# Retention, Mish layer and GELU layer in one kernel: from unit 7 on, the scores of two units stand in a row

## The chip, the cores and the metric

The kernel runs on one core of a Trainium2 chip. The metric is device time in microseconds (us) of one launch, the median of several runs. The engines are named as in the profile: PE (TensorE's matmuls) and PEld (its weight loads), DVE (VectorE), ACT (ScalarE), POOL (GpSimd) and SP (SyncE, which issues the DMAs).

## The reference, cut to what matters

```python
scores = scale * np.matmul(q, k.transpose(0, 1, 3, 2))      # B, H, S, D = 4, 8, 576, 64
...
Dmat = np.where(rel >= 0, gamma[:, None, None] ** rel[None, :, :], 0.0)
ret = scores * Dmat[None, :, :, :]
return np.matmul(ret, v).astype(np.float32)
...
h = x @ w_in                                                # 2304 x 512 by 512 x 2048
g = h * np.tanh(sp)                                         # Mish
return (g @ w_out).astype(np.float32)
...
g = h * (1.0 / (1.0 + np.exp(-1.702 * h)))                  # the second layer, same sizes
return (g @ w_out).astype(np.float32)
```

A retention (attention with a decay in place of a softmax), and behind it two feed-forward layers. The change is in the retention alone.

## The kernel before, in words

**Units.** Retention is worked off in 20 units, numbered u = 0 to 19: four batches of five stretches of the sequence, four of 128 positions and a last one of 64 (the rests: units 4, 9, 14 and 19). A unit's q, k and v lie in one of six buffers (`unit` in the profile: three of the kernel's own with numbers 76 to 78, three lent by the layers that come later) or, for a rest, in `rest`. Within a batch a unit takes over a state from the unit before it.

**What PE does for a unit.** Four groups of eight float32 matmuls each, one per head. The profile counts 16 records for a group of eight.

- `sc` (L875, in `scores`): the products of q and k. They go to two PSUM banks, one for the even heads and one for the odd ones. A weight tile has 64 rows and 128 columns (64 and 64 for a rest).
- `ds` (L898, in `update`): the unit's addition to the state, summed in a bank that the units of a batch share. A rest has none. ACT copies the sum to `state` (in `take`) before the next unit may add to it.
- `o` from `state` (L926, in `outputs`): what the state of before gives. The first unit of a batch has none.
- `o` from `pm` (L938, in `outputs`): masked scores times v. The `ds` and `o` groups have weight tiles of 128 rows and 64 columns, but for the last group of a rest, which has 64 and 64.

**What the other engines do for a unit.** DVE multiplies the two banks of scores with a causal mask into two tiles `pm` (L879, the masks: two instructions); a unit's banks are free for other scores when its masks have read them. When `o` is complete DVE multiplies it with a table into `X` (L956, in `finish`). Between these DVE stands in the service of the coming layers: it splits `X` into two parts (L403), and converts weights (L202, L142, L214, L250), with ACT and POOL. All engines work off their instructions in the order of the program.

**Banks.** Scores take turns in four banks, two per unit (`bank("sc", (0, 1, 2, 3))`). So the scores of unit u+2 use the banks of unit u.

**The order.** It is written out by hand in the loop over u in `attention`: from unit 4 on a step of the loop issues the scores and masks of u+1, then `ds` of u, `o` of u, `finish` of u, and then what is planned of conversions. At the end of steps 17 and 18 the first products of the next layer (`h`, L416) are issued.

Of the kernel before, what the change touches and what calls it, by code (L numbers as in the profile page):

```python
# [25 lines left out]
CH = [(c, min(P, S - c)) for c in range(0, S, P)]  # L26
NCH = len(CH)
UNITS = [(b, c) for b in range(B) for c in range(NCH)]
# [19 lines left out]
LAG = 3  # L48

KEPT = (0, 1, 2, 3, 4, 8, 9, 10, 11, 12)  # L50
X_UNITS = (4, 5, 6, 7, 10, 11, 12, 13)
EARLY_AT = ((2, 8), (7, 13))
EARLY = len(EARLY_AT)
# [47 lines left out]
def retention_mish_gelu_kernel(ctx: ExitStack, tc: tile.TileContext, qkv, w1, w2, first_unit, rests, out):  # L101
# [23 lines left out]
    def bank(kind, of):  # L125
        taken[kind] = taken.get(kind, -1) + 1
        return ps.tile([P, NB], F32, tag=f"b{of[taken[kind] % len(of)]}", name=kind)

    def quarters(t):
        return t.rearrange("p (c n) -> p c n", c=NPAIR)  # L130

    def act(o, i, f=AF.Copy, scale=1.0, bias=0.0):
        nc.scalar.activation(out=o, in_=i, func=f, scale=scale, bias=bias)  # L133
# [18 lines left out]
    def plan(name, step, job):  # L152
        plans.setdefault(name, []).append((step, job))
        plans[name].sort(key=lambda p: p[0])

    def position(name, step):
        for j in [j for j in under_way if j[1] == name]:
            j[1] = next(j[0], None)
            if j[1] is None:
                under_way.remove(j)  # L160
        while plans.get(name) and plans[name][0][0] <= step:
            job = plans[name].pop(0)[1]
            then = next(job, None)
            if then:
                under_way.append([job, then])
# [8 lines left out]
    def place(m):  # L174
        return keep if m in KEPT else late[0]

    def fetch(m):

        r, h = divmod(m, 2)
        for i in range(2):  # L180
            if h == 0:
                at = RAW[i, r]
                held[i, r] = place(at).tile([P, 4, DM // 2], I64, tag=f"w{at}", name="raw")
            nc.sync.dma_start(
                out=held[i, r][:, 2 * h : 2 * h + 2],
                in_=w1[m][:, i * DM : (i + 1) * DM].rearrange("p (q n) -> p q n", q=2),
            )
        return
        yield
# [173 lines left out]
    n_u = len(UNITS)  # L363
# [12 lines left out]
    for m, s in zip(range(EARLY, NM), LATE):  # L376
        here = m < NM - 2 and all(RAW[i, m // 2] in KEPT and RAW[i, m // 2] not in LENT for i in range(2))
        plan("fetch", s - 2.5 if here else max(s - 2.5, 0), fetch(m))
# [417 lines left out]
    def attention():  # L796
        with tc.tile_pool(name="att", bufs=1) as ap:
# [11 lines left out]
            def load(u):  # L809

                b, c = UNITS[u]
                if c == NCH - 1:
                    t = ap.tile([P, LAST], F32, tag="rest", name="rest", bufs=2)
                    nc.sync.dma_start(out=t, in_=rests[b])
                    loaded[u] = views(t, REST)
                    return
                t = buffers[(u - b) % len(buffers)]
                if u == 0:
                    for e0, e in ((0, 2 * DM), (2 * DM, FIRST)):
                        nc.sync.dma_start(out=t[:, e0:e], in_=first_unit[:, e0:e])  # L820
                else:
                    for e in (0, 2 * DM) if u == 1 else (0,):
                        e1 = e + 2 * DM if u == 1 else 4 * DM
                        nc.sync.dma_start(out=t[:, e:e1], in_=qkv[b, c, :, e:e1])
                loaded[u] = views(t, P)
# [34 lines left out]
            def decay_v(u):  # L860
                b, c = UNITS[u]
                n = CH[c][1]
                vv = loaded[u][2][:n].rearrange("p (h d) -> p h d", d=D)
                for eng, h, e in ((nc.vector, 0, SPLIT), (nc.gpsimd, SPLIT, H)) if u == 0 else ((nc.gpsimd, 0, H),):
                    by = vt[:n, c, h:e].unsqueeze(2).to_broadcast([n, e - h, D])
                    eng.tensor_tensor(out=vv[:, h:e], in0=vv[:, h:e], in1=by, op=ALU.mult)

            def scores(u):
                n = CH[UNITS[u][1]][1]
                qt, kt = loaded[u][:2]  # L870
                sc = [quarters(bank("sc", (0, 1, 2, 3))) for _ in range(2)]
                for p in range(NPAIR):
                    for j in range(2):
                        sl = slice(64 * j, 64 * j + 64)
                        nc.tensor.matmul(sc[j][:n, p, :n], lhsT=kt[sl, p, :], rhs=qt[sl, p, :], start=True, stop=True)  # L875
                pm[u] = []
                for j in range(2):
                    t = ap.tile([P, NPAIR, P], F32, tag="pm", name="pm", bufs=4)
                    nc.vector.tensor_tensor(  # L879
                        out=t[:n, :, :n],  # L880
                        in0=sc[j][:n, :, :n],
                        in1=cm[:n, :n].unsqueeze(1).to_broadcast([n, NPAIR, n]),
                        op=ALU.mult,
                    )
                    pm[u].append(t)

            def update(u):

                c = UNITS[u][1]
                if c == NCH - 1:  # L890
                    return
                v, kk = loaded[u][2:]
                if c == 0:
                    sums[0] = quarters(bank("ds", (4, 5)))
                for p in range(NPAIR):
                    for j in range(2):
                        sl = slice(p * P + 64 * j, p * P + 64 * j + 64)
                        nc.tensor.matmul(  # L898
                            sums[0][64 * j : 64 * j + 64, p, :D],
                            lhsT=kk[:, sl],  # L900
                            rhs=v[:, sl],
                            start=(c == 0 and p == 0),
                            stop=True,
                            skip_group_check=True,
                        )

            def take(u):

                if UNITS[u][1] == NCH - 1:
                    return None  # L910
                for j in range(2):
                    sl = slice(64 * j, 64 * j + 64)
                    act(state[u % 2][sl, :, sl], sums[0][sl, :, :D])
                return state[u % 2]
# [55 lines left out]
            for u in range(n_u):  # L970
                step = u - n_u
                if u - 1 in wide and wide.index(u - 1) + len(buffers) < len(wide):
                    n = wide[wide.index(u - 1) + len(buffers)]
                    load(n)
                    if n + 1 not in wide:
                        load(n + 1)
                if u + 1 < n_u:
                    decay_v(u + 1)
                position("pool", step)
                position("fetch", step)  # L980
                if u == 0:
                    for n in wide[NCH : len(buffers)]:
                        load(n)
                if NCH - 1 <= u < n_u - 1:
                    scores(u + 1)
                before = now[0]

                def step_state():
                    update(u)
                    now[0] = take(u)  # L990

                if u != 1:
                    step_state()
                o = outputs(u, before, *((step_state,) if u == 1 else ()))
                if 0 < u < NCH - 1:
                    scores(u + 1)
                if u < NCH - 1:
                    n = CH[u + 1][1]
                    for p in range(NPAIR):
                        act(gt[:, u + 1, p, :n], gt[:, 0, p, :n], scale=steps[:, p, u + 1 : u + 2])  # L1000
                position("act early", step)

                if u == n_u - 2:
                    elementwise(0, jobs=False)
                finish(u, o)
                if u == n_u - 1:
                    elementwise(1, jobs=False)
                if u == 0:
                    scores(1)
                position("vector", step)  # L1010
                position("act late", step)
                if u in X_UNITS:
                    k = X_UNITS.index(u)
                    split_x((0, SIDE)[k // NK], k % NK)()
                if u == n_u - 3:
                    up(0)
                if u == n_u - 2:
                    up(1)
# [266 lines left out]
```

## Time and profile before

| what | value |
|---|---|
| median of 3 runs | 807.77 us (807.33 to 807.77) |
| the profiled execution | 807.27 us, of which 805.6 us are its span |
| PE busy | 800.3 us, 99% of the span |
| DVE busy | 585.9 us, 73% |
| ACT, POOL busy | 446.3 us, 55%; 190.3 us, 24% |
| retention on PE | from 4.8 us to 70 us of the span |
| PE's idle time that another engine ended | 0.5 us at the first `ds`, 0.4 us at 480 us |

The share of busy time is a mean over stages. For the retention alone the stretch from 13 to 70 us has to be looked at; in the 25 us from 35 to 60 DVE is as busy as PE. A PE that is busy all the time has not the same speed all the time: how long a group of matmuls takes from its first start to the first start of the next group is read from the order of time.

### The profile page before, as it was taken

The page shows a single profiled execution, that of the slowest core. Times are in us where ns is not written, and L with a number is a line of the kernel's source. Part 1 is how long each engine was busy: PE and PEld are TensorE (multiplying, and loading weights), DVE is VectorE, ACT ScalarE, POOL GpSimd, SP SyncE. Part 2 cuts the span into 40 slices and gives each one's busy share as a digit, 9 for nine tenths or more (in the row PEclk, how much of TensorE's full clock was granted, in tenths as well). Part 3 has the DMA queues.
Part 4 walks back from the last instruction along what each step waited for, and adds up shares of the span by engine and source line. Part 5 has one row for each costly group of instructions (what it writes and reads, how often), then busy time and mean ns, then how long its engine had stood idle before and what let it go on. Part 6 is the DMA issues. An engine that isn't in the chain of part 4 may idle for free.

```text
span 805.6 us, 14286 instructions
## 1 busy us (share of the span) xinstructions
PE 800.3 (99%) x5394; PEld 760.9 (94%) x5394; DVE 585.9 (73%) x992; ACT 446.3 (55%) x861; POOL 190.3 (24%) x251
## 2 busy tenths in 40 slices
PE   9999999999999999999999999999999999999998
PEld 8998888889999999999999999999999999999998
DVE  4896999998687666577677376798555897656775
ACT  5455877766766665666566454664233663234542
POOL 3362322220376450366570051000000000000000
PEclk9999999999999999999999999999999999999999
DMA  9994578837789995698986699888888788888784
GB/s 367 416 376 132 192 266 277 279 127 245 276 298 332 311 318 177 210 325 309 346 284 217 206 347 382 272 273 266 298 252 256 249 273 287 280 251 257 254 267 161
DMA packets 92326, 219.68 MB, mean 273 GB/s; under 512 B 6497, under 2 KB 52577, under 8 KB 90465
## 3 DMA queue, kind: packets, MB, share of 16 engines
q1 hardware_dynamic: 92112, 218.56, 80.4%
q8 instruction: 43, 0.70, 0.3%
q14 instruction: 27, 0.21, 0.1%
q10 hardware_dynamic: 144, 0.20, 0.1%
HBM read 169.98 MB, written 48.76 MB: 272 GB/s over the span
## 4 chain that ended last, share of the span: by engine, by line
PE 98%; DVE 1%; DMA 1%; ACT 0%; issue 0%; SPq 0%
PE p L731 22%; PE p L682 21%; PE acc L1093 17%; PE p L1156 15%; PE h L416 8%; PE acc L437 8%; PE sc L875 2%; PE o L938 2%; PE o L926 2%; PE ds L898 1%; DMA unit<-first_unit_dram 1%; DVE cs L475 0%; DVE u L475 0%; DVE X L142 0%; ACT cs L133 0%; DVE cy L352 0%
## 5 line engine op out<-in xcount | busy, mean ns | idle before, releaser
L682 PE MATMUL p<-xop,ring 128*128 128x384 f32 x1008 | 175.6, 334 | 0.4 <-DVE cs L475 0.4
L682 PEld LDWEIGHTS p<-xop,ring 128*128 128x128 f32 x1008 | 174.6, 188 | 0.8 <-DVE cs L475 0.7
L731 PE MATMUL p<-g,ring 128*128 128x384 f32 x1008 | 175.2, 334 | 0.0
L731 PEld LDWEIGHTS p<-g,ring 128*128 128x128 f32 x1008 | 174.8, 188 | 0.0
L1093 PE MATMUL acc<-g,w 128*128 128x512 f32 (+1 forms) x768 | 143.8, 337 | 0.0
L1093 PEld LDWEIGHTS acc<-g,w 128*128 128x128 f32 x768 | 124.3, 188 | 17.1 <-DVE g L475 0.3
L1156 PE MATMUL p<-xop,ring 128*128 128x384 f32 x672 | 128.4, 337 | 0.0
L1156 PEld LDWEIGHTS p<-xop,ring 128*128 128x128 f32 x672 | 115.7, 188 | 0.3
L133 ACT ACTIVATE g<-cs 128x384 fp32r<-128x384 f32 x168 | 79.0, 517 | 60.3 <-PE p L731 60.0
L475 DVE TENSOR_TENSOR g<-cs,g 128x384 fp32r<-128x384 f32 x168 | 90.0, 553 | 26.7 <-ACT g L133 25.1
L133 ACT ACTIVATE cs<-cs 128x384 f32<-128x384 f32 x72 | 37.8, 526 | 104.6 <-DVE cs L475 104.6
L475 DVE TENSOR_TENSOR g<-c,g 128x384 fp32r<-128x384 f32 x64 | 44.0, 688 | 39.0 <-ACT g L133 38.2
L437 PE MATMUL acc<-g,w 128*128 128x512 f32 (+1 forms) x384 | 72.3, 337 | 0.0
L437 PEld LDWEIGHTS acc<-g,w 128*128 128x128 f32 x384 | 60.2, 190 | 7.6
L133 ACT ACTIVATE c<-p 128x384 f32<-128x384 f32 x64 | 31.3, 489 | 54.4 <-PE p L1156 54.0
L218 POOL TENSOR_TENSOR raw<-raw 128x512 int32<-128x512 int32 x32 | 37.2, 1161 | 97.1 <-DVE raw L214 85.6
L133 ACT ACTIVATE g<-c 128x384 fp32r<-128x384 f32 (+1 forms) x96 | 50.5, 526 | 12.4 <-PE acc L437 9.9
L342 POOL TENSOR_TENSOR cy<-cy 128x128 f32<-128x128 f32 x88 | 54.9, 634 | 5.2
L475 DVE TENSOR_TENSOR cs<-cs 128x384 f32<-128x384 f32 x96 | 53.4, 556 | 0.8
L133 ACT ACTIVATE raw<-raw 128x512 int32<-128x512 uint32 x64 | 42.1, 680 | 16.7 <-DVE raw L202 16.7
L416 PE MATMUL h<-x,w 128*128 128x512 f32 x192 | 46.4, 391 | 0.0
L218 POOL TENSOR_TENSOR cy<-cr 128x256 int32<-128x256 int32 x38 | 31.2, 842 | 62.0 <-DVE cr L214 57.4
(93 smaller groups left out, 963.4 us busy)
## 6 DMA issues: line engine op xcount, KB each, us to landing
ring<-stream SPq DMA_DIRECT2D x168, 512.0 KB, 4.6
ring<-first_stream SPq DMA_DIRECT2D x56, 512.0 KB, 5.3
stream<-cy SPq DMA_DIRECT2D x22, 896.0 KB, 5.2
raw<-w_dram SPq DMA_DIRECT2D x32, 512.0 KB, 8.3
unit<-qkv_dram SPq DMA_DIRECT2D x14, 1024.0 KB, 13.7
cr<-w_dram SPq DMA_DIRECT2D x19, 512.0 KB, 5.7
stream<-X SPq DMA_DIRECT2D x10, 896.0 KB, 5.3
first_stream<-cy SPq DMA_DIRECT2D x16, 512.0 KB, 3.3
```

Of the source, the lines that this page charges most:

```text
L133: nc.scalar.activation(out=o, in_=i, func=f, scale=scale, bias=bias)
L218: nc.gpsimd.tensor_tensor(out=o, in0=upper, in1=bits, op=ALU.add)
L342: nc.gpsimd.tensor_tensor(out=v[:, o], in0=v[:, a], in1=v[:, b], op=op)
L416: nc.tensor.matmul(h[:, :n], lhsT=W[0, m // 2][:, m % 2, a, k * P : (k + 1) * P], rhs=xs[t, k][:, b, :n], start=((k, a, b) == order[0]), s ...
L437: nc.tensor.matmul(acc[t, e][:, :n], lhsT=W[1, m // 2][:, m % 2, a, e * P : (e + 1) * P], rhs=g[:, b, :n],  start=(begins(i) and a == 0 an ...
L475: eng.tensor_tensor(out=o, in0=a, in1=b, op=op)
L682: nc.tensor.matmul(banks[p], lhsT=w[:, k, a * P : (a + 1) * P], rhs=x[:, b, k], start=(p not in SAME and k == 0 and a == 0 and b == 0), st ...
L731: nc.tensor.matmul(banks[e, p], lhsT=w[:, e, a * P : (a + 1) * P], rhs=g[:, b], start=(p != 2 and r == 0 and a == 0 and b == 0), stop=(r = ...
L875: nc.tensor.matmul(sc[j][:n, p, :n], lhsT=kt[sl, p, :], rhs=qt[sl, p, :], start=True, stop=True)
L926: nc.tensor.matmul(o[sl, p, :n], lhsT=before[:, p, sl], rhs=qt[:, p, :], start=(p == 0), stop=True, skip_group_check=True,)
L1093: nc.tensor.matmul(acc[t, e][:, :w], lhsT=W[1, m // 2][:, m % 2, a, e * P : (e + 1) * P], rhs=g[:, b, o : o + w], start=(m == 0 and a == 0 ...
L1156: nc.tensor.matmul(bank, lhsT=w[:, a, k * P : (k + 1) * P], rhs=x[:, b, k], start=(p in (1, 2, 7) and k == 0 and a == 0 and b == 0), stop= ...
```

## The change

`scores` is split into products and masks. From step 7 on every second step issues the products and masks of unit u+1 and at once the products of unit u+2; the step behind it issues only the masks of its u+1 (whose products are there already). So the products of units 8 and 9 stand in a row, then those of 10 and 11, and so on to 18 and 19: six pairs. Behind each pair the `ds` and `o` groups of two units follow one another.

```diff
+PAIRS_FROM = 7
...
-            def scores(u):
+            products = {}
+
+            def scores(u, mask=True):
                 n = CH[UNITS[u][1]][1]
                 qt, kt = loaded[u][:2]
-                sc = [quarters(bank("sc", (0, 1, 2, 3))) for _ in range(2)]
+                sc = products[u] = [quarters(bank("sc", (0, 1, 2, 3))) for _ in range(2)]
                 for p in range(NPAIR):
                     for j in range(2):
                         sl = slice(64 * j, 64 * j + 64)
                         nc.tensor.matmul(sc[j][:n, p, :n], lhsT=kt[sl, p, :], rhs=qt[sl, p, :], start=True, stop=True)
+                if mask:
+                    masks(u)
+
+            def masks(u):
+                n = CH[UNITS[u][1]][1]
+                sc = products.pop(u)
                 pm[u] = []
...
-                if NCH - 1 <= u < n_u - 1:
+                if u >= PAIRS_FROM and (u - PAIRS_FROM) % 2 and u < n_u - 1:
+                    masks(u + 1)
+                elif NCH - 1 <= u < n_u - 1:
                     scores(u + 1)
+                    if PAIRS_FROM <= u < n_u - 2:
+                        scores(u + 2, mask=False)
```

On DVE, ACT, POOL and SP the instructions stand in the same order as before. On PE, this is the middle of the stretch before, from the scores of unit 12 to the last group of unit 13 (`unit` without a number is a lent buffer; the unit of batch 2 with the rest is 14):

```order
L875 MATMUL sc<-unit 128x128 x8
L898 MATMUL ds<-unit 64x64 x8
L926 MATMUL o<-unit,state_72 64x128 x8
L938 MATMUL o<-pm,unit 64x128 x8
L875 MATMUL sc<-unit 128x128 x8
L898 MATMUL ds<-unit 64x64 x8
L926 MATMUL o<-unit,state_73 64x128 x8
L938 MATMUL o<-pm,unit 64x128 x8
L875 MATMUL sc<-rest 64x64 x8
L898 MATMUL ds<-unit 64x64 x8
L926 MATMUL o<-unit,state_72 64x128 x8
L938 MATMUL o<-pm,unit 64x128 x8
```

And the same place of the changed kernel, whose lines have other numbers (L878 for L875, L907 for L898, L935 for L926, L947 for L938):

```order
L878 MATMUL sc<-unit 128x128 x16
L907 MATMUL ds<-unit 64x64 x8
L935 MATMUL o<-unit,state_72 64x128 x8
L947 MATMUL o<-pm,unit 64x128 x8
L907 MATMUL ds<-unit 64x64 x8
L935 MATMUL o<-unit,state_73 64x128 x8
L947 MATMUL o<-pm,unit 64x128 x8
L878 MATMUL sc<-rest 64x64 x8
L878 MATMUL sc<-unit_76 128x128 x8
L907 MATMUL ds<-unit 64x64 x8
L935 MATMUL o<-unit,state_72 64x128 x8
L947 MATMUL o<-pm,unit 64x128 x8
```

The scores of 13 now stand ahead of the three groups of unit 11, and those of 15 (`unit_76`) ahead of the three groups of unit 13.

The second place is PE's where the first product of the next layer (`h`) lies within the retention; before:

```order
L416 MATMUL h<-x_494,w_622 128x512
L875 MATMUL sc<-rest 64x64 x8
L898 MATMUL ds<-unit 64x64 x8
L926 MATMUL o<-unit,state_73 64x128 x8
L938 MATMUL o<-pm,unit 64x128 x8
L416 MATMUL h<-side,w_622 128x256 x12
```

and with the change:

```order
L417 MATMUL h<-x_504,w_622 128x512
L907 MATMUL ds<-unit 64x64 x8
L935 MATMUL o<-unit,state_73 64x128 x8
L947 MATMUL o<-pm,unit 64x128 x8
L417 MATMUL h<-side,w_622 128x256 x12
```

The scores of unit 19, the last rest, have left this place; they stand behind those of unit 18, ahead of unit 17's groups and of `h`.

## Rows read from the trace of the kernel before

**Rows 1.** Windows: busy us of each engine in three stretches, and granted clock (PEclk)

```profile
35.00:60.00 25.00, 25.00 (x492) 22.66 (x490) 24.79 (x45) 13.33 (x28) 14.15 (x13) 1.00 0.95 392
...
230.00:430.00 200.00, 200.00 (x1141) 186.32 (x1141) 136.78 (x200) 124.77 (x225) 101.53 (x147) 1.00 0.87 291
430.00:806.00 376.00, 371.66 (x2143) 369.08 (x2141) 256.13 (x477) 171.31 (x350) 14.92 (x24) 1.00 0.81 264
```

**Rows 2.** Timeline of PE: start us, us, what, tile rows*columns, xrecords

```profile
10.64 0.64 PE L898 MATMUL ds<-unit 128*64 128x64 f32 x16
11.11 1.14 PE L938 MATMUL o<-pm,unit 128*64 128x128 f32 x16
...
28.26 1.16 PE L875 MATMUL sc<-unit 64*128 64x128 f32 x16
29.35 0.69 PE L898 MATMUL ds<-unit 128*64 128x64 f32 x16
29.86 1.05 PE L926 MATMUL o<-unit,state 128*64 128x128 f32 x16
30.74 1.04 PE L938 MATMUL o<-pm,unit 128*64 128x128 f32 x16
31.71 0.68 PE L875 MATMUL sc<-rest 64*64 64x64 f32 x16
32.32 0.69 PE L898 MATMUL ds<-unit 128*64 128x64 f32 x16
...
52.89 0.69 PE L898 MATMUL ds<-unit 128*64 128x64 f32 x16
...
61.29 3.03 PE L416 MATMUL h<-x,w 128*128 128x512 f32 x12
64.25 0.68 PE L875 MATMUL sc<-rest 64*64 64x64 f32 x16
64.86 0.69 PE L898 MATMUL ds<-unit 128*64 128x64 f32 x16
```

**Rows 3.** Timeline of DVE, units 7 to 17: start us, us, what, [idle before]

```profile
31.83 0.69 DVE L956 TENSOR_TENSOR X<-o,gt 128x512 f32<-128x512 f32 x1 [0.91 <-PE o L938]
...
33.76 0.74 DVE L879 TENSOR_TENSOR pm<-sc,cm 64x256 f32<-64x256 f32 x2
...
37.64 0.41 DVE L956 TENSOR_TENSOR X<-o,gt 128x256 f32<-128x256 f32 x1
...
39.36 1.27 DVE L879 TENSOR_TENSOR pm<-sc,cm 128x512 f32<-128x512 f32 x2
...
43.82 0.68 DVE L956 TENSOR_TENSOR X<-o,gt 128x512 f32<-128x512 f32 x1
...
45.07 1.26 DVE L403 TENSOR_TENSOR side<-X,side 128x256 fp32r<-128x256 f32 x1
46.26 1.27 DVE L879 TENSOR_TENSOR pm<-sc,cm 128x512 f32<-128x512 f32 x2
...
48.65 0.41 DVE L403 TENSOR_TENSOR side<-X,side 128x256 fp32r<-128x256 f32 x1
...
49.65 0.67 DVE L956 TENSOR_TENSOR X<-o,gt 128x512 f32<-128x512 f32 x1
...
50.92 1.27 DVE L879 TENSOR_TENSOR pm<-sc,cm 128x512 f32<-128x512 f32 x2
...
55.78 0.70 DVE L142 SCALAR_TENSOR_TENSOR raw<-raw 128x512 int32<-128x512 int32 x1
...
56.86 1.28 DVE L879 TENSOR_TENSOR pm<-sc,cm 128x512 f32<-128x512 f32 x2
```

**Rows 4.** Timeline of ACT: the copy of the state's sum behind unit 15's products

```profile
53.68 0.78 ACT L133 ACTIVATE state<-ds 64x256 f32<-64x256 f32 x2 [2.28 <-PE ds L898]
```

**Rows 5.** Timeline of POOL: two of its decays of v, which DMAs or its own work precede

```profile
35.19 1.04 POOL L866 TENSOR_TENSOR unit<-unit,unit 128x512 f32<-128x512 f32 x1 [1.90 <-DMA unit<-qkv_dram]
...
44.56 1.48 POOL L866 TENSOR_TENSOR rest<-rest,unit 64x512 f32<-64x512 f32 x1
```

## The prediction

> **What bounds the kernel now.** I read the windows first. From 35 to 60 us, inside the retention, PE is busy 25.00 of 25.00 us at full granted clock, and DVE 24.79; from 230 to 430 us PE is busy all the time and DVE 137 of 200; in the last 376 us PE lacks 4.3 [rows 1]. So the end is set by PE, and what PE gains or loses in the retention reaches the end almost whole; but in the middle of the retention DVE has nothing to spare, and that is where the change moves PE's work. Then I read PE's order of time, for what a group costs between its neighbours, and DVE's, for when the masks and the `finish` of each unit come.
>
> **What a group costs, start to start.** A `ds` between groups of its own tile shape (128 rows*64 columns) takes 11.11 - 10.64 = 0.47 us. Behind scores it takes 29.86 - 29.35 = 0.51, and the scores of a rest, of the same width but with another shape on both sides, 32.32 - 31.71 = 0.61. An `o` followed by `o` takes 30.74 - 29.86 = 0.88, an `o` followed by scores 31.71 - 30.74 = 0.97 [rows 2]. So a change of tile shape costs 0.10 us at the end of the old shape and 0.05 at the first pass of the new one, 0.15 in all, where the new tiles are 64 wide. Scores of a whole unit take 29.35 - 28.26 = 1.09 [rows 2] with a change at either side. Their 16 records pass as many columns as those of an `o`, so I take 0.88 for them alone; 0.10 is the end, and 0.11 is left for their first pass: 0.21 for a change into them.
>
> The Trainium skill, "TensorEngine Tiling (Array Packing)", section Tiling Modes, says that a change of the tiling mode drains TensorE, while other tiles of one mode run on. The 0.10 us agree. By that rule alone the change could only gain; that is a rival below.
>
> **What the change takes away.** I count the changes of shape on PE from the scores of unit 8 to the first `h`, and on to the end of the retention, from the two orders: 25 before, 18 with the change. Of the seven that go, three lead into scores of whole units (units 11, 13 and 17 now follow scores of their own shape): 3 x 0.21 = 0.63. Four lead into 64-wide groups: 4 x 0.15 = 0.60. Together 1.2 us. No instruction is added, none is taken away, and the DMA queue keeps its order. The load of unit 11 is the one that the earlier scores come near to: POOL began on that unit at 35.19, released by its DMA [rows 5], and the scores of 11 would start at 35.5. I cost it at nothing; a load later than that would show in the same place.
>
> **What it adds: waits for banks.** The scores of the second unit of a pair, u+2, write the banks of u, which DVE's masks of u must have read. Before, they stood behind the `o` of u, which needs these masks anyway. Now they stand ahead of `ds` and `o` of u, and DVE, which has kept its order, has often not got there. I follow the clock of before, group by group, with the prices above.
>
> *Units 8, 9.* Scores 8 start at 28.26 as before, 9 at 29.35, `ds` 7 at 29.96, `o` at 30.47 and 31.35, `ds` 8 at 32.23 (before 32.32 [rows 2]). The masks of 7 were done long before: no wait. `finish` 7 starts some 0.1 us behind the end of the last `o` (31.83 against 31.71 before [rows 2, 3]), so at 32.35, 0.5 late.
>
> *Units 10, 11.* `o` 8 at 32.70 and 33.58, scores 10 at 34.55, scores 11 wanted at 34.55 + 0.11 + 0.88 = 35.54. The masks of 9 ended at 33.76 + 0.74 = 34.50 [rows 3], 0.5 later now: no wait. `o` 9 at 36.52 and 37.13, `ds` 10 at 37.74. `finish` 9 then starts at 37.86 in place of 37.64 [rows 3]; DVE is 0.22 late, and has no idle time from here to 55 us in which to catch up.
>
> *Units 12, 13.* `o` 10 at 38.26, scores 12 at 39.23, 13 wanted at 40.22. The masks of 11 ended at 39.36 + 1.27 = 40.63 [rows 3], now at 40.85: **0.63 us of waiting**. It ends with the second of the two banks, and behind it a whole group with a fresh first pass is still to come: 1.09, not 0.98. `ds` 11 starts at 41.94. The loss is 0.63 + 0.11 = 0.74.
>
> *Units 14, 15.* `o` 11 at 42.45 and 43.33, `ds` 12 at 44.21. `finish` 11 cannot start before 44.33; it did at 43.82 [rows 3]. DVE is 0.51 late. `o` 12 at 44.68 and 45.56, scores 14 at 46.53, 15 wanted at 47.14. The masks of 13 ended at 46.26 + 1.27 = 47.53, now 48.04: **0.90 us**; `ds` 13 starts at 49.13.
>
> *Units 16, 17.* `o` 13 at 49.64 and 50.52, `o` 14 at 51.40. `finish` 13 starts at 51.52 against 49.65 [rows 3]: DVE is 1.87 late. `o` 14 of the rest takes 0.57 and 0.61, scores 16 start at 52.58, 17 is wanted at 53.57. The masks of 15 ended at 50.92 + 1.27 = 52.19, now 54.06: **0.49 us**, and 0.11 for the first pass; `ds` 15 starts at 55.15.
>
> *`ds` 16.* Unit 15 is the first of a batch and has one `o` group only, so `ds` 16 is wanted 0.51 + 0.88 later, at 56.54. ACT has the sum copied 53.68 + 0.78 - 52.89 = 1.57 us after the start of `ds` 15 [rows 2, 4], at 56.72: **0.18 us**. Behind that copy on ACT stand its conversions, for which DVE's L142 (55.78 before [rows 3]) waits.
>
> *Units 18, 19.* `ds` 16 at 56.72, `o` at 57.19 and 58.07, scores 18 at 59.04, 19 wanted at 60.13. The masks of 17 ended at 56.86 + 1.28 = 58.14 [rows 3], now at 60.01, or up to 0.3 later where L142 waited for ACT: 0 to 0.2, I take 0.1. `ds` 17 at 60.84, `o` at 61.35 and 62.23, `h` at 63.20. `h` takes 64.25 - 61.29 = 2.96 and has the scores of 19 behind it no more: `ds` 18 at 66.16, before 64.86 [rows 2]. **1.3 us later.** From here both kernels have the same order.
>
> As a sum: 0.74 + 0.90 + 0.60 + 0.18 + 0.10 = 2.5 lost, less 1.2 gained. The profiled execution then takes 807.27 + 1.3 = 808.6 us, and the median of the runs shown, 807.77, becomes 809.1. I predict 809.0, between the two.
>
> **The bounds.** What I cannot price is where DVE and POOL meet. The same L403 took 0.41 us at 48.65 and 1.26 at 45.07 [rows 3], where a POOL instruction ran from 44.56 to 46.04 [rows 5]: DVE's instruction ends 0.3 us after POOL's. The Trainium skill, "SBUF — State Buffer", section SBUF: two separate sides, calls it an exclusive lock, which whoever comes first holds for its whole instruction; the rows agree. With DVE shifted by 0.2 to 1.9 us, each such meeting is drawn anew. One more or one less ahead of a mask that PE waits for is 0.85 us. If one falls away, and the fresh first pass costs nothing, the change costs 1.3 - 0.85 - 0.22 = 0.2; if one is added, and ACT's 0.3 us count in full, it costs 1.3 + 0.85 + 0.3 = 2.5. In medians, 808.0 to 810.3. A measurement of this kernel can tell some 0.2%, 1.6 us, from no change.
>
> **The rivals.**
>
> *Slower by more than that: the waits feed themselves.* Place: `finish` 13, the step where DVE goes from 0.5 to 1.9 late. A `finish` waits for `o`, the masks behind it wait for the `finish`, the next scores for the masks. If one more meeting with POOL, or a longer start behind a wait, falls between 41 and 56 us, it goes through all later pairs. It decides from 0.3 us over my sum; with one meeting of 0.85 it gives 810.0. For it: DVE's 24.79 of 25.00 us [rows 1]. Against it: collisions can fall away as well.
>
> *The gain alone.* DVE is in time and the seven changes of shape are saved: 807.77 - 1.2 = 806.6. That is the time by the rule of the tiling page. For it: PE waits for nothing before. Against it: the scores of 15 would have to start 0.4 us before the masks of 13 end even on the clock of before (47.1 against 47.53).
>
> *Little of either.* One meeting with POOL falls away in the stretch from 45 to 48 us, waits and gain are about equal: 808.0.
>
> **How the numbers follow.** My sum 0.60 (from 1.0 to 1.9 us later, a third of it beyond 1.6), the waits that feed themselves 0.25, the gain alone 0.06, little of either 0.09. Slower by over 0.2%: 0.25 + 0.18 = 0.43. Faster by over 0.2% needs more than 1.6 us, and the gain is 1.2: 0.02. Within 0.2%: 0.55. The range leaves out the gain alone and the far end of the first rival: 807.6 to 810.3.
>
> **What would show it.** In the profile of the changed kernel: PE with idle time before the scores of units 13, 15 and 17, ended by DVE's masks, 0.5 to 0.9 us each, none at 9 and 11; DVE with a new idle time of over 1 us before the `finish` of 13; an `o` of 0.88 ahead of a `ds`, and no 0.10 us between the scores of 12 and 13; `ds` 18 near 66.2 us. The prediction is wrong if these waits are absent (DVE is then not what holds the banks), if the order of the middle comes out right and the end doesn't follow (some wait further on then took the shift up), or if unit 11's load is awaited.

## The result, and the profile after

The changed kernel takes 812.54 us (median of 4 runs: 812.65, 812.62, 810.36, 812.46) against 807.75 of the kernel before beside it: a ratio of 1.0054, 95% interval 1.0037 to 1.0072. That is slower, by 4.8 us where I forecast 1.3, and outside my range. Two later groups of five runs give 1.0036 (1.0023 to 1.0049) and 1.0047 (1.0035 to 1.0060). The fourteen runs are of two kinds: six have a mean granted clock of 0.998 and lie between 812.5 and 812.7, the other eight have 0.999 or 1.000 and lie between 809.1 and 811.1, with a median of 810.2. The profiled execution (812.65 us, span 810.9) is one of the six.

The windows of the kernel after, the first one as in [rows 1] (PE, PEld, DVE, ACT, POOL busy, then the granted clock):

```profile
35.00:60.00 25.00, 23.37 (x406) 21.25 (x404) 20.15 (x38) 9.71 (x21) 9.13 (x9) 0.93 0.95 392
...
51.00:52.00 1.00, 1.00 (x21) 1.00 (x22) 0.99 (x3) 0.06 (x1) 0.00 (x0) 0.69 0.89 373
52.00:53.00 1.00, 1.00 (x14) 1.00 (x12) 0.00 (x0) 0.95 (x3) 0.00 (x0) 0.50 1.03 426
...
54.00:55.00 1.00, 1.00 (x16) 1.00 (x14) 0.00 (x0) 0.00 (x0) 0.00 (x0) 0.61 1.07 430
55.00:56.00 1.00, 1.00 (x34) 0.93 (x30) 0.87 (x2) 0.00 (x0) 0.00 (x0) 1.00 0.98 393
```

PE was busy 25.00 of the 25 us and is now busy 23.37; DVE falls from 24.79 to 20.15. And PE was at full clock throughout; now it stands at the half level (1.2 GHz, 0.50 in the row) from about 51.4 to 54.8, worked out from the 0.69 and the 0.61 at the two ends. Two different losses, then: idle time, and a slow stretch in which PE counts as wholly busy.

PE's order of time after, from the first scores to the `ds` of unit 18, to be held against [rows 2]:

```profile
4.95 2.08 PE L878 MATMUL sc<-unit 64*128 64x128 f32 x16
...
29.13 1.16 PE L878 MATMUL sc<-unit 64*128 64x128 f32 x16
...
40.11 1.61 PE L878 MATMUL sc<-unit 64*128 64x128 f32 x18
41.91 1.13 PE L878 MATMUL sc<-unit 64*128 64x128 f32 x14 [0.19 <-DVE pm L888]
42.97 0.69 PE L907 MATMUL ds<-unit 128*64 128x64 f32 x16
...
47.55 0.68 PE L878 MATMUL sc<-rest 64*64 64x64 f32 x16
49.30 0.46 PE L878 MATMUL sc<-unit 64*128 64x128 f32 x2 [1.07 <-issue]
49.95 1.13 PE L878 MATMUL sc<-unit 64*128 64x128 f32 x14 [0.19 <-DVE pm L888]
51.00 0.84 PE L907 MATMUL ds<-unit 128*64 128x64 f32 x16
51.62 1.93 PE L935 MATMUL o<-unit,state 128*64 128x128 f32 x16
...
54.92 0.63 PE L935 MATMUL o<-rest,state 128*64 128x64 f32 x16
...
56.09 1.56 PE L878 MATMUL sc<-unit 64*128 64x128 f32 x18
57.84 1.13 PE L878 MATMUL sc<-unit 64*128 64x128 f32 x14 [0.18 <-DVE pm L888]
58.89 0.69 PE L907 MATMUL ds<-unit 128*64 128x64 f32 x16
59.41 1.04 PE L947 MATMUL o<-pm,unit 128*64 128x128 f32 x16
60.61 0.69 PE L907 MATMUL ds<-unit 128*64 128x64 f32 x16 [0.16 <-ACT state L134]
...
70.18 0.69 PE L907 MATMUL ds<-unit 128*64 128x64 f32 x16
```

Read it from the starts. `ds` 18 starts 5.32 us later than before (70.18 against 64.86), and the span is 5.3 us longer: everything happens ahead of it and reaches the end whole. Of these, 0.87 were there before the change does anything: the first scores took 2.08 us in place of 1.16, and the scores of unit 8 start at 29.13 in place of 28.26. From those scores to `ds` 18 it is **41.05 us against 36.60**, 4.45 more. This stretch is the measure that I use for all runs below, since the start varies from one execution of a kernel to the next.

The waits stand where they were forecast: at the scores of 13, 15 and 17, and at `ds` 16. That at unit 15 is far the largest. The profile puts its 1.07 us down to "issue"; what DVE did tells more. DVE and then POOL after (compare [rows 3] and [rows 5]):

```profile
45.45 0.69 DVE L965 TENSOR_TENSOR X<-o,gt 128x512 f32<-128x512 f32 x1 [0.44 <-PE o L947]
46.06 2.20 DVE L251 TENSOR_TENSOR w<-raw,w 128x512 fp32r<-128x512 f32 x1
48.19 0.41 DVE L404 TENSOR_TENSOR side<-X,side 128x256 fp32r<-128x256 f32 x1
48.52 1.28 DVE L888 TENSOR_TENSOR pm<-sc,cm 128x512 f32<-128x512 f32 x2
...
55.13 0.69 DVE L965 TENSOR_TENSOR X<-o,gt 128x512 f32<-128x512 f32 x1 [3.14 <-PE o L947]
```

```profile
44.67 1.04 POOL L867 TENSOR_TENSOR unit<-unit,unit 128x512 f32<-128x512 f32 x1
45.67 1.04 POOL L867 TENSOR_TENSOR rest<-rest,unit 64x512 f32<-64x512 f32 x1
46.67 1.04 POOL L867 TENSOR_TENSOR unit<-unit 128x512 f32<-128x512 f32 x1
```

The conversion line L251 took 2.20 us, 1.5 more than its 0.67 a few us later; it ends 0.55 us after the last of three POOL instructions that stand back to back. The masks of unit 13 stand behind it, from 48.52 to 49.80, and the scores of 15 start as these free their banks. Then the clock falls, the two `o` of 13 take 3.3 us (51.62 to 54.92) where they take 1.75 at full clock (51.12 to 52.87 in a later profile of the same kernel, below), and `finish` 13 at 55.13 has waited 3.14 us.

### The profile page after: what moved, and what is told of

The parts are those of the page before. It is cut to its first block, busy times and chain, and to the rows that moved or that the text cites. A ratio compares the mean times of both kernels' runs of the same rounds, so it can differ in the third digit from the quotient of the medians.

```text
span 810.9 us, 14283 instructions
## 1 busy us (share of the span) xinstructions
PE 804.2 (99%) x5394; PEld 764.6 (94%) x5394; DVE 585.4 (72%) x992; ACT 446.2 (55%) x861; POOL 191.5 (24%) x251
## 4 chain that ended last, share of the span: by engine, by line
PE 97%; DVE 2%; ACT 0%; issue 0%; ACTq 0%; DVEq 0%
PE p L732 22%; PE p L683 20%; PE acc L1106 17%; PE p L1169 15%; PE h L417 8%; PE acc L438 8%; PE sc L878 2%; PE o L947 2%; PE o L935 2%; PE ds L907 1%; DVE pm L888 1%; PE unused L853 1%; DVE cs L476 0%; DVE X L965 0%; DVE u L476 0%
```

## The experiments

The table gives for each kernel the median, its ratio to the kernel before on the same chip (95% interval), how long the first scores took in its profiled execution, and there the time from the scores of unit 8 to `ds` 18, beside the 36.60 us of before.

| kernel | median us | ratio | first scores us | sc 8 to ds 18 us |
|---|---|---|---|---|
| before (first profile) | 807.77 | | 1.16 | 36.60 |
| changed (first profile) | 812.54 | 1.0054 (1.0037 to 1.0072) | 2.08 | 41.05 |
| changed, again | 810.30 | 1.0036 (1.0023 to 1.0049) | 1.69 | 39.43 |
| changed, third time | 811.14 | 1.0047 (1.0035 to 1.0060) | 1.53 | 39.40 |
| changed, filled | 810.73 | 1.0041 (1.0027 to 1.0055) | 2.08 | 39.61 |
| filled, again | 810.41 | 1.0037 (1.0024 to 1.0049) | 1.72 | 39.67 |
| changed, no scaling of 14, 15 | 809.12 | 1.0018 (1.0009 to 1.0027) | 2.08 | 37.87 |
| changed, POOL held | 809.07 | 1.0017 (1.0008 to 1.0026) | 2.08 | 37.87 |
| changed, less on DVE | 807.94 | 1.0003 (0.9994 to 1.0012) | 2.08 | 36.58 |
| all pairs but 14/15 | 808.71 | 1.0015 (1.0006 to 1.0024) | 1.16 | 37.93 |
| pairs 8/9 and 10/11 alone | 807.84 | 1.0001 (0.9992 to 1.0010) | 1.16 | 37.01 |
| these two, POOL held | 807.15 | 0.9996 (0.9987 to 1.0005) | 2.00 | 36.26 |
| 8/9, 10/11, 14/15, POOL held | 807.36 | 1.0000 (0.9991 to 1.0009) | 1.16 | 36.43 |
| before, POOL held | 807.61 | 0.9999 (0.9990 to 1.0008) | 1.46 | 36.61 |

**Two pairs alone.**

```diff
-PAIRS_FROM = 7
+PAIRS = (7, 9)
...
-                if u >= PAIRS_FROM and (u - PAIRS_FROM) % 2 and u < n_u - 1:
+                if u - 1 in PAIRS:
...
-                    if PAIRS_FROM <= u < n_u - 2:
+                    if u in PAIRS:
```

> Only units 8 and 9, and 10 and 11, are paired; later units stand as before the change. Theory (waits at full banks set the loss, and the clock's fall follows from the largest of them): in these two pairs no scores waited for masks, and the trace after showed a gain of 0.35 us up to the state products of unit 10, so 807.4 us, the granted clock 1.00 from 35 to 60, the half clock of 3.4 us gone. Rival (the loss is at the start, where the first scores ran at half clock, and comes with the changed program whatever is paired): 0.87 us later from the first scores on, 808.3 us.

807.84 us, ratio 1.0001: no change that can be told, 0.4 over the theory. The first scores took 1.16 us in this profile, so the rival does not hold in it. The gain came and was lost again further on. `ds` 10 lies 0.35 us ahead of before, counted from the scores of 8 (37.79 - 28.30 = 9.49 against 38.10 - 28.26 = 9.84), `ds` 11 still 0.35; but then (DVE, POOL and PE of this kernel):

```profile
44.84 1.48 POOL L867 TENSOR_TENSOR rest<-rest,unit 64x512 f32<-64x512 f32 x1
...
45.35 2.26 DVE L404 TENSOR_TENSOR side<-X,side 128x256 fp32r<-128x256 f32 x1
...
46.29 1.03 POOL L867 TENSOR_TENSOR unit<-unit 128x512 f32<-128x512 f32 x1
...
48.86 1.09 PE L947 MATMUL o<-pm,unit 128*64 128x128 f32 x14 [0.16 <-DVE pm L888]
```

DVE's split (L403 before, 1.26 us in [rows 3]) now took 2.26, through two POOL instructions instead of one; the masks of 13 came late, and the `o` of 13 waited for them. What made the meeting longer is open: DVE's split starts 0.51 us after POOL's scaling of the rest here (45.35, 44.84), as it did before (45.07, 44.56 [rows 3, 5]); there DVE came in between two POOL instructions, here it stood through both.

**All pairs but 14/15.** The edit is against the kernel with two pairs.

```diff
-PAIRS = (7, 9)
+PAIRS = (7, 9, 11, 15, 17)
```

> All pairs but that of units 14 and 15, whose scores stand apart as before. Theory: the wait of 1.07 us at the scores of unit 15 and the half clock after it go; the waits of 0.19 us at unit 13 and 0.18 at unit 17 stay, and the pairs' gain of some 1.0 us too: 807.0 to 808.0 us, granted clock 1.00 from 35 to 60. Rival (each wait, or the sum of the small ones, is enough for the clock to fall): a stretch at 0.50 after unit 13 or unit 17 and 809 to 810 us.

808.71 us, 1.1 us over before, 0.7 over the upper end of the theory; no run of 11 below 0.999 in clock. The wait at 15 and the half clock are gone, as the theory had it, but the waits at 13, 17 and `ds` 16 cost more than the idle time that stands beside them in the rows (0.19, 0.18 and 0.16 in the changed kernel): see the sum below.

**The idle time filled.**

```diff
+FILL = 8
...
+            def fill(n):
+                o = ps.tile([P, NB], F32, tag=f"b{(6, 7)[(taken['o'] + 1) % 2]}", name="unused")[:, :P]
+                for _ in range(n):
+                    nc.tensor.matmul(o, lhsT=zeros, rhs=zeros, start=True, stop=True)
...
                     scores(u + 1)
+                    if u == 13:
+                        fill(FILL)
                     if PAIRS_FROM <= u < n_u - 2:
                         scores(u + 2, mask=False)
```

> The change, with 8 more products of 128 columns of zeros (0.85 us at full clock) between the scores of unit 14 and those of unit 15, where TensorE stood idle 1.07 us. Theory (the idle time there lets the clock fall, which costs 1.65 us at the two groups of outputs behind it): the clock stays at 1.00 and the time falls to 810.9 us, though nothing is taken from any wait. Rival (the clock falls for another reason, or the waits at 49.95 and after do it alone): 812.5 us, or up to 0.3 us more for the filling.

810.73 us. PE's order of time in this kernel:

```profile
48.15 2.05 PE L875 MATMUL unused<-const-float32-0.0 128*128 128x128 f32 x16
50.13 1.16 PE L885 MATMUL sc<-unit 64*128 64x128 f32 x16
51.22 0.69 PE L914 MATMUL ds<-unit 128*64 128x64 f32 x16
51.73 1.05 PE L942 MATMUL o<-unit,state 128*64 128x128 f32 x16
```

The eight products took 2.0 us, over twice what I had reckoned, and `ds` 13 starts 0.2 us later than with the change alone. The granted clock stays at 1.00, both `o` of 13 take 1.05, and the median is 1.8 us under that of the first four runs of the change (0.7 under it on one chip, below). Useless work in the place of idle time paid in the mean of all runs, 810.7 us in 10 against 811.2 in 14; where the clock stays up without it, it costs 0.2 us (39.61 against 39.43 in the table).

**GpSimd's scaling of two units left out.**

```diff
-                if u + 1 < n_u:
+                if u + 1 < n_u and u + 1 not in (14, 15):
                     decay_v(u + 1)
```

> The change without GpSimd's scaling of the values of units 14 and 15 (left out of the computation), which ran back to back from 44.67 to 47.71 while VectorE's conversion line took 2.20 us instead of 0.73. Theory (GpSimd's work makes that line long, the line makes the masks of unit 13 late, these the scores of unit 15, and that idle time the clock's fall): the line takes 0.7 us, scores of unit 15 start 1 us or more earlier, the clock stays at 1.00, 812.5 - 1.5 - 1.65 = 809.4 us. Rival 1 (only the meeting goes, the clock still falls): 811.0 us. Rival 2 (the masks are late by VectorE's queue order alone): 812 us or more.

809.12 us against 809.4. L251 takes 0.68 us, the scores of 15 start at 48.15 without idle time ahead of them, the wait is down from 1.75 to 0.24 us, the clock stays up.

**The changed kernel again.**

> The changed kernel once more, unaltered, beside the kernel before. The first scores' half clock (2.08 us instead of 1.16, 0.87 us to everything behind) was in three of the profiles with every pair and in none of the two with fewer, and the runs of one kernel lie in two clusters some 0.7 us apart. Theory (this start falls out by chance in any kernel; the fall of the clock after unit 15's scores belongs to the change): times between 811.6 and 812.7 us, the fall in nearly all runs, median 812.3. Rival (the start belongs to the changed program): all at 812.5 but for single ones without the fall.

Neither the theory nor its rival gives these times, 809.1 to 812.5 us with a median of 810.3: by its mean clock one run of five had the fall, far from nearly all. The profiled execution is one without it (PE):

```profile
4.95 1.69 PE L878 MATMUL sc<-unit 64*128 64x128 f32 x16
...
48.90 0.46 PE L878 MATMUL sc<-unit 64*128 64x128 f32 x2 [1.06 <-issue]
...
50.60 0.69 PE L907 MATMUL ds<-unit 128*64 128x64 f32 x16
51.12 1.05 PE L935 MATMUL o<-unit,state 128*64 128x128 f32 x16
...
52.87 0.63 PE L935 MATMUL o<-rest,state 128*64 128x64 f32 x16
```

The same idle time of 1.06 us, and `o` at full speed behind it. So the idle time does not bring the fall by itself. The first scores took 1.69 us where the first profile of this very kernel had 2.08: the start differs between executions of one kernel, as the theory said.

**POOL held, in three kernels.** A copy of one column makes POOL wait for DVE's split of unit 11 before it scales the rest 14; here in the kernel before, in that with two pairs, and further below in the change itself.

```diff
+                if u == 14:
+                    nc.gpsimd.tensor_copy(out=column[:, 1:2], in_=side[-1][:, 1, 1, :1].bitcast(F32))
```

> The kernel before, with GpSimd's scaling of unit 14's values held until VectorE's split of unit 11 is written (a copy of one column ahead of it). In the kernel before VectorE's split took 1.26 us instead of 0.41 there, and TensorE waited for nothing. Theory: the meeting goes and nothing is gained, 807.3 to 807.8 us. Rival (TensorE's pace hung on it unseen): 806.8 us.

807.61 us: the split takes 0.41 us, the meeting of [rows 3] is gone, and nothing is gained, as the theory had it. PE did not depend on it before.

> Units 8 and 9, and 10 and 11 paired, with the same hold of GpSimd's scaling of unit 14. With those two pairs alone VectorE's split took 2.26 us, since two of GpSimd's scalings stood back to back on it, and the outputs of unit 13 started 0.7 us late. Theory (the pairs' gain of 0.35 us was given back there): the split takes 0.42 us, no output waits, 0.7 us less than with the two pairs alone: 807.1 us, faster than both kernels. Rival (the meeting only moves on, to VectorE's next lines): 807.8 us.

807.15 us, 0.6 under before on the same chip and 0.7 under the two pairs alone (on another chip), as forecast, though the interval (0.9987 to 1.0005) does not tell it from the kernel before. The profiles do, one of each: 36.26 us in place of 36.60, in an execution whose first scores took 2.00. Here the gain of two pairs holds, where DVE meets no two POOL instructions in a row ahead of masks that PE waits for. The meeting did move on, as the rival says (L251 takes 2.07 us at 48.24), to a place where nobody waits.

**Less work on DVE.**

```diff
-        sign(raw)
+        if m >= EARLY:
+            sign(raw)
...
-        nc.vector.tensor_tensor(out=lo, in0=value, in1=hi.bitcast(F32), op=ALU.subtract)
+        if m >= EARLY:
+            nc.vector.tensor_tensor(out=lo, in0=value, in1=hi.bitcast(F32), op=ALU.subtract)
+        else:
+            act(lo, value)
```

> The change with VectorE's sign lines and its subtraction left out for the two early weights (a ScalarE copy stands in its place), which leaves part of their conversion out. VectorE loses about 2.6 us for each of the four halves that fall in retention. Theory (the masks come late because VectorE is full, so each wait at a bank goes with its load): no wait of TensorE for masks, the clock at 1.00, 806.6 us, or 807.4 with the half clock at the start. Rival (the masks are late because they stand behind finish in VectorE's order, one unit later, full or not): the waits at the scores of units 13 and 17 stay at 0.4 to 0.9 us each, 808 to 809 us.

807.94 us, between the two, and each holds in its place. PE in this kernel, and DVE's `finish` 13:

```profile
40.11 2.06 PE L882 MATMUL sc<-unit 64*128 64x128 f32 x32
42.09 0.69 PE L911 MATMUL ds<-unit 128*64 128x64 f32 x16
...
46.67 0.68 PE L882 MATMUL sc<-rest 64*64 64x64 f32 x16
47.28 1.16 PE L882 MATMUL sc<-unit 64*128 64x128 f32 x16
48.37 0.69 PE L911 MATMUL ds<-unit 128*64 128x64 f32 x16
...
50.85 0.69 DVE L969 TENSOR_TENSOR X<-o,gt 128x512 f32<-128x512 f32 x1 [2.39 <-PE o L951]
...
51.81 1.56 PE L882 MATMUL sc<-unit 64*128 64x128 f32 x18
53.56 1.13 PE L882 MATMUL sc<-unit 64*128 64x128 f32 x14 [0.18 <-DVE pm L892]
54.61 0.69 PE L911 MATMUL ds<-unit 128*64 128x64 f32 x16
55.13 1.04 PE L951 MATMUL o<-pm,unit 128*64 128x128 f32 x16
56.33 0.69 PE L911 MATMUL ds<-unit 128*64 128x64 f32 x16 [0.16 <-ACT state L134]
```

At 13 and 15 no wait is left: 42.09 - 40.11 = 1.98 us for two groups of scores in a row, 48.37 - 46.67 = 1.70 for a rest and a whole unit. At 13 a full DVE was the cause. At 15 this run can't tell DVE's load from its meeting with POOL, since the edit also takes away the L251 that met POOL; the held kernel below does. At 17 the wait stays, 54.61 - 51.81 = 2.80, so 0.82 us, though DVE is idle 2.39 us ahead of `finish` 13: there it is the order. The masks of 15 stand behind `finish` 13, which waits for `o` 13, and only the short `o` of the rest lies between that and the scores of 17.

**Again, on one chip: the change, the filled one and the held one.**

> The changed kernel a third time, beside the filled one and the held one, on one chip. So far 4 of its 9 runs had a mean granted clock of 0.998 and lay near 812.5 us, the others between 809.1 and 810.6. Theory (idle time before unit 15's scores makes the fall likely, not certain): some runs again near 812.5, the rest near 810. Rival (the fall belonged to the first chip's moment): all near 810.

Two runs of five at 0.998 and 812.6, the others 810.0, 810.2 and 811.1, as the theory had it.

> The change with 8 products of zeros ahead of unit 15's scores, again, since the fall is now known to come in some runs only. They took 2.0 us there and not 0.85, so that the state products of unit 13 came 0.2 us later than with the change alone. Theory (no idle time, no fall): no run at 0.998 and all between 810.2 and 811.3 us. Rival (the first five were luck): one or more runs near 812.7.

810.3 to 810.9 us, none at 0.998. Together, by the mean clock: six falls in 14 runs with the idle time of 1.07 us, none in 10 with it filled, none in the 32 runs of the three kernels that keep the waits at 13 and 17 but not that at 15 as it was (no scaling, POOL held, without 14/15). Among the 87 runs of the kernel before, which has no such idle time in its profile, there is one at 0.998, with 809.67 us.

> The change with GpSimd's scaling of unit 14's values held until VectorE's split of unit 11 is written; nothing is left out. Theory (the back-to-back scalings are what made the wait at unit 15's scores 1.75 us in place of 0.9): VectorE's conversion line takes 0.73 us instead of 2.20, the scores of unit 15 wait 0.2 us, no fall, 808.4 to 809.4 us. Rival (what is left slower has nothing to do with the scalings): 810 us or more.

809.07 us with nothing left out, within 0.1 of the kernel without the scalings, and the same 37.87 us. All engines of this kernel:

```profile
46.05 0.68 DVE L251 TENSOR_TENSOR w<-raw,w 128x512 fp32r<-128x512 f32 x1
...
47.14 0.18 POOL L866 COPY column<-side 128x1 f32<-128x1 f32 x1 [1.44 <-DVE side L404]
47.27 1.04 POOL L869 TENSOR_TENSOR rest<-rest,unit 64x512 f32<-64x512 f32 x1
...
47.54 0.68 PE L880 MATMUL sc<-rest 64*64 64x64 f32 x16
48.15 1.39 PE L880 MATMUL sc<-unit 64*128 64x128 f32 x16
...
49.47 0.69 PE L909 MATMUL ds<-unit 128*64 128x64 f32 x16
```

The wait is 49.47 - 47.54 - 1.70 = 0.23 us in place of 1.75. So it is POOL's place in time, not its work, that made 1.5 us of the wait of unit 15.

**One pair more.** The edit is against the held kernel with two pairs.

```diff
-PAIRS = (7, 9)
+PAIRS = (7, 9, 13)
```

> Units 8 and 9, 10 and 11, and 14 and 15 paired, with the hold of GpSimd's scaling of unit 14. The two pairs alone, held, lay 0.34 us ahead of the kernel before at the state products of unit 18, counted from the scores of unit 8. Theory (the wait at unit 15's scores came from unit 13's masks standing one unit later; with units 12 and 13 apart they are done in time): no wait at unit 15 over 0.1 us, another 0.15 us gained, 0.5 us ahead there, 806.9 to 807.1 us. Rival (the pair 14 and 15 waits by itself, for masks of 13 that are written as late as TensorE reaches it): 0.2 us or less ahead, 807.3 us or more.

The rival holds: 807.36 us, 0.17 us ahead over the stretch instead of 0.34. The scores of 15 take 1.38 us at 46.83 and not 1.16, since the masks of 13 (45.73 to 47.01) free their banks as PE arrives. In these two profiles the pair 14/15 costs more than it saves even with POOL held; the medians, on two chips, can't tell.

## Why the prediction was wrong, step by step

Each wait is measured from start to start against the same groups without a wait (1.98 and 1.70 in the kernel with less on DVE; from `ds` 13 to the `o` of the rest 52.87 - 50.60 = 2.27 in the changed kernel without the fall; 0.88 for an `o` ahead of its own shape, as in the prediction). The `ds` of 17 came 64.87 - 64.07 = 0.80 us after the scores of 19, against 60.40 - 59.78 = 0.62 there.

| term | forecast | measured, changed kernel |
|---|---|---|
| scores 13 | 0.74 | 42.97 - 40.11 - 1.98 = 0.88 |
| scores 15 | 0.90 | 51.00 - 47.55 - 1.70 = **1.75** |
| scores 17 | 0.60 | 58.89 - 56.09 - 1.98 = 0.82 |
| `ds` 16 | 0.18 | 60.61 - 59.41 - 0.88 = 0.32 |
| scores 19 | 0.10 | 0.80 - 0.62 = 0.18 |
| changes of shape | -1.2 | -1.16 |
| half clock in `o` 13 | none | 54.92 - 51.00 - 2.27 = **1.65** |
| sum | 1.3 | 4.44, of 4.45 |

The sum is bound to close nearly, since the gain and three of the prices come from one kernel, that with less on DVE.

**What bounds the kernel: right.** PE's shift in the retention reached the end whole, and none of it was taken up.

**The gain: right.** The kernel with less on DVE has lost 0.82 at 17 and 56.33 - 55.13 - 0.88 = 0.32 at `ds` 16 and is 0.02 us ahead over the stretch, so the gain is 1.16. For the first two pairs alone it was 0.35 at `ds` 10, where the clock that I followed has 0.36. By the rule of the Trainium skill that the prediction goes by in its second rival ("TensorEngine Tiling (Array Packing)", section Tiling Modes) the change could only gain; the waits decided.

**Where the waits are: right.** None at 9 and 11, one each at 13, 15, 17, 16 and 19, in this order. That `ds` 16 would wait for ACT, and DVE's L143 for the conversion behind it (0.59 us idle at 61.80), came as told. So did the cause at 17, the masks of 15 behind a `finish` 13 that waits for `o` 13: with less work on DVE, and DVE idle for 2.39 us there, that wait is the same 0.82. But the four waits at 13, 17, 16 and 19 are 0.1 to 0.2 us longer each, 0.58 in all. At least in part that is time that the prediction put at nothing or too short: PE goes on 0.15 us after the masks end (49.80 to 49.95), and `finish` 11 starts 0.22 us behind the next group of PE (45.45 against 45.23) in place of 0.12.

**The first step that failed: the wait at the scores of 15, 0.90 us.** I took DVE's work between `finish` 11 and the masks of 13 at the length that it had before, and kept "one more" meeting of 0.85 for the bounds and for the first rival, with 0.25. The wait was 1.75, and without the back-to-back scalings, or with POOL only held, it is 0.24 and 0.23. That it is just 0.85 more is luck. From the start of `finish` 11 to the end of the masks of 13 DVE took 49.80 - 45.45 = 4.35 us, before 47.53 - 43.82 = 3.71 [rows 3]: 0.64 more, because the meeting of 0.85 at the split fell away and one of 1.5 came at L251. The other 0.2 are the late starts just named.

The first rival came nearest: a meeting between 41 and 56 us, and 810.0 us, where the eight runs without the fall of the clock have a median of 810.2. But it did not go through all later pairs: the waits at 17, 16 and 19 are 0.82, 0.32 and 0.18 us with POOL held too. The likelihood of the meeting was in view: three POOL scalings follow one another there in the profile before too, at 43.56, 44.56 [rows 5] and 46.05, and DVE was to arrive 0.5 us late in their midst. (In the chances, a third of the 0.60 is 0.20, and I added 0.18.)

The Trainium skill, "SBUF — State Buffer", section SBUF: two separate sides, says that a DVE instruction with two SBUF inputs and a GpSimd instruction that reads SBUF contend for one pair of ports, and that whoever starts first has it for the whole instruction. These rows agree (the masks, with one input in PSUM, took 1.27 us at 46.26 [rows 3] beside POOL, and 1.28 at 56.41 in the changed kernel without it) and add that the price isn't always one instruction: 2.20 and 2.26 us went by while two of POOL's ran. In other profiles DVE came in between the two (its conversion line took 1.20 us without 14/15, 1.21 in the second filled one), and its split then met the second of POOL's (1.26 us in both).

**The second step that failed: PE at full clock.** The prediction took the work behind the idle time at full clock, a term put at nothing. In six of 14 runs the mean clock shows a fall; in the one of them that was profiled the idle time of 1.07 and 0.19 us was followed by a stretch at 1.2 GHz that cost 1.65 us more. The median of the first four runs is among these, and without the fall the runs lie about the upper end of my range, 810.3. Filling the idle time, or taking its cause away in three ways, left no fall in 42 runs, so the link is shown; why it falls in some runs and not in others is open. Two things more are open: the six runs lie 2.4 us over the median of the other eight and not 1.65, and one run, of 809.08 us, lies a microsecond under all others of the changed kernel.

**The start.** 0.87 us of the first profile's 5.3 arise before the change does anything. The changed kernel's first scores took 2.08, 1.69 and 1.53 us in its three profiles (in the third the first `ds` then waited 0.98 us for DVE), and 1.46 in that of the kernel before with POOL held. The eight profiles with all six pairs have the scores of unit 8 at 28.74 us or later, and five of the other six at 28.54 or earlier, so that chance alone is not shown. But over many runs it matters little: with less on DVE the scores of unit 8 came 0.86 us late in the profile, and the median is only 0.2 us over the kernel before, at the same stretch.

## What to carry to other kernels

When an order is changed on the engine that bounds, list for each engine that answers it which of its instructions can be stretched by a neighbour, and price the next step of that stretch as likely, not as a bound, where the neighbour's instructions stand back to back. Where a buffer is wanted a unit earlier, its reader must be done a unit earlier too: in the first two pairs it was, and they gained 0.34 us over the stretch; each of the four behind them waited. Idle time of a microsecond ahead of dense work may cost more than itself, as here in six of 14 runs: hold the work that makes it, or, if nothing else helps, fill it.

## What the runs showed of the hardware that was not expected

- After idle time of 1.07 and 0.19 us PE's granted clock stood at 1.2 GHz in place of 2.4 for some 3.4 us (51.4 to 54.8 us) in the profile. By the mean clock of 0.998 six of 14 runs had such a fall, none of 42 without that idle time, and one of the 87 of the kernel before.
- The first scores took from 1.16 to 2.08 us, and 1.53 to 2.08 in three profiles of one kernel, while the row of granted clock stood at 1.00 in these windows; so the "half clock" that the expectations name there is not shown.
- Eight float32 products of 128 columns took 2.0 us where PE would have been idle 1.26, and the median fell by 0.7 us on the same chip.
- When a DVE instruction met two POOL instructions in a row, it stood through one of them or through both, with nothing in its own time to tell which: in the two profiles of the filled kernel the conversion line took 2.20 and 1.21 us, and started 0.39 us behind POOL's scaling of the rest in both.
